# First up-projection slice of a SwiGLU kernel: from two hardware-queue loads to one load issued by GpSimd

## The chip, the cores and the metric

The kernel runs on one core of one Trainium2 chip. The metric is the device time of one execution in microseconds; of several executions the median is given. A profile is one execution taken by the hardware profiler. Its span runs from the first to the last instruction that the profile shows.

In the profile's lines, PE is TensorE (matmul), PEld its weight loads, DVE VectorE, ACT ScalarE, POOL GpSimd, SP SyncE. "SPq" and "ACTq" stand for an engine's issuing of transfers. `L195` is line 195 of the kernel before.

## The reference

```python
def reference(x, w_gate, w_up, w_down):
    g = _silu(x @ w_gate)
    u = x @ w_up
    return (g * u) @ w_down
```

x is 2048 x 640, w_gate and w_up are 640 x 1536, w_down is 1536 x 640, all bf16, and so is the output of 2048 x 640.

## The kernel before, in words

The 2048 rows are worked in four blocks of 512 (`NSB`, `S_BLK`). For a block, the gate and up projections come first, with the result transposed: the 1536 features lie on partitions in 12 tiles of 128 (`fc`), the 512 rows along the free dimension. One such tile is five matmuls for the gate (`pg`, over the five 128-row pieces `kd` of the inner dimension 640) and five for up (`pu`), both in `proj` (L195). `gate` then applies silu on ScalarE (L212) and multiplies on VectorE (L213) into `aT`. After 12 tiles the down projection runs from `aT` and `wd_sb` (L270 for the last 128 output columns, L299 for the first 512), and the results are stored. VectorE works out the last four rows of the output's inner products by itself (L148, `row_dots`) beside the other work.

The matmuls need x with its inner dimension on partitions (`xT`). Most of it comes through crossbar loads, transfers that transpose on their way (`turn_x`, L110, issued by SyncE, 512 rows at a time). The first 256 rows of block 0 (`PE_X` = 2 pieces of 128) come otherwise: they are loaded plainly into `x_sb` (L86), turned on TensorE with an identity matrix (L186), and copied to `xT` by ScalarE and VectorE (L191). The other 256 rows of block 0 come through the first crossbar load (L121 calls `turn_x(PE_X, SUB)`).

The weights come in slices of feature tiles, `W_CHUNKS` = (0, 2), (2, 4), (4, 8), (8, 12). The first slice of gate and up (256 columns, 320 KB each: 128 partitions x 5 pieces x 512 bytes) is split by `kd` at `K_CUT` = 2 between two queues, L115 to L120:

- gate, pieces 0 and 1 (128 KB): SyncE; pieces 2 to 4 (192 KB): ScalarE
- up, pieces 0 and 1 (128 KB): ScalarE; pieces 2 to 4 (192 KB): SyncE

After that SyncE issues, in this order: the first crossbar load, the remaining six weight slices (L83), w_down (L126), the crossbar load of block 1, and the transposed weights for VectorE's part. ScalarE goes on with its activation table and a first silu (L122).

`head` writes out the start of block 0. PE runs 18 small matmuls on ones (`warm`, L177), the ten transposes of x (L186), two more small matmuls, and then the gate matmuls of feature tiles 0 and 1 over the first 256 rows (L237, 14 of them: for pieces 0 and 1 in two halves of 128 rows, for pieces 2 to 4 over 256 rows). Then come the up matmuls of the same tiles and rows (L244, L245: ten, from `wu_sb`), and then, for each of the two tiles, the gate and up matmuls of the other 256 rows, which need the first crossbar load. From there on every tile is whole. `keep_order(engine)` ties each instruction of an engine to the one before it, in the order of the program; in `head` it is called for PE and ScalarE, at the end for VectorE and SyncE. GpSimd has only small memsets and the making of the identity (L71), at the very start.

`_trim` takes barriers out of the start and the end of the program and leaves the closing to SyncE.

Of the kernel before, what the change touches and what calls it, by code (L numbers as in the profile page):

```python
# [10 lines left out]
def _body(  # L11
# [8 lines left out]
    nc = tc.nc  # L20
# [12 lines left out]
    KD = D // P  # L33
# [10 lines left out]
    K_CUT = 2  # L44
    ROW_J = 0
    W_CHUNKS = [(0, 2), (2, 4), (4, 8), (8, 12)]
# [12 lines left out]
    wg_sb = consts.tile([P, KD, F], bf16)  # L59
    wu_sb = consts.tile([P, KD, F], bf16)  # L60
# [14 lines left out]
    wg_v = w_gate.rearrange("(kd p) f -> p kd f", p=P)  # L75
    wu_v = w_up.rearrange("(kd p) f -> p kd f", p=P)
    wd_v = w_down.rearrange("(kf p) d -> p kf d", p=P)

    def wslice(a, b):
        return slice(a * P, b * P)  # L80

    def load_w(eng, dst, src, a, b):
        eng.dma_start(out=dst[:, :, wslice(a, b)], in_=src[:, :, wslice(a, b)])  # L83
# [4 lines left out]
    def issue_order(a, b):  # L88
        tc.add_manual_dep(
            b,  # L90
            a.name,
            mybir.DependencyInfo(
                mybir.DependencyClass.NoSync, mybir.DependencyReason.DATA
            ),
            reason="issue_order",
        )

    def keep_order(engine):

        traced = [i for i in nc.cur_bb.bb.instructions if i.engine == engine]  # L100
        for a, b in zip(traced, traced[1:]):
            issue_order(a, b)
# [5 lines left out]
    def turn_x(c0, c1):  # L108
        s_sl = slice(c0 * P, c1 * P)
        nc.sync.dma_start_transpose(out=xT[:, :, s_sl], in_=xt_v[s_sl])  # L110
# [1 line left out]
    load_x(nc.sync, 0, 1)  # L112
    load_x(nc.scalar, 1, 2)
    f_sl = wslice(*W_CHUNKS[0])
    for dst, src, first, second in (  # L115
        (wg_sb, wg_v, nc.sync, nc.scalar),
        (wu_sb, wu_v, nc.scalar, nc.sync),
    ):
        for eng, k_sl in ((first, slice(0, K_CUT)), (second, slice(K_CUT, KD))):
            eng.dma_start(out=dst[:, k_sl, f_sl], in_=src[:, k_sl, f_sl])  # L120
    turn_x(PE_X, SUB)  # L121
    nc.scalar.activation(silu_first[:], ones[:, 0:1], ACT.Silu)  # L122
    for a, b in W_CHUNKS[1:]:
# [6 lines left out]
    def turn_w(dst, src):  # L130
# [7 lines left out]
        out=x_row[:],  # L138
        in_=x2[S - T : S, :].rearrange("t d -> (t d)").partition_broadcast(P),
# [35 lines left out]
    def warm(n):  # L175
        for _ in range(n):
            nc.tensor.matmul(  # L177
                pw[:, 0:P], lhsT=ones[:], rhs=ones[:], start=True, stop=True
            )

    def transpose_chunk(c, parts):
        c_sl = slice(c * P, (c + 1) * P)
        for copy, tag, k0, k1 in parts:
            pt = psum.tile([P, k1 - k0, P], bf16, tag=tag, name="pt")
            for kd in range(k0, k1):
                nc.tensor.transpose(  # L186
                    out=pt[:, kd - k0, :],
                    in_=x_sb[:, c, kd * P : (kd + 1) * P],
                    identity=ident[:],
                )  # L190
            copy(out=xT[:, k0:k1, c_sl], in_=pt[:])  # L191

    def proj(ps, w_sb, fc, sb, c0, c1):
        for kd in range(KD):
            nc.tensor.matmul(  # L195
                ps[:, c0:c1],
                lhsT=w_sb[:, kd, fc * P : (fc + 1) * P],
                rhs=xT[:, kd, sb * S_BLK + c0 : sb * S_BLK + c1],
                start=(kd == 0),
                stop=(kd == KD - 1),  # L200
            )

    def gu_tiles():
        pg = psum.tile([P, S_BLK], f32, tag="gu", name="pg", bufs=4)
        pu = psum.tile([P, S_BLK], f32, tag="gu", name="pu", bufs=4)
        return pg, pu

    def gate(pg, pu, sb, fc, n_s):

        s0 = sb * S_BLK  # L210
        sg = work.tile([P, S_BLK], f32, name="sg")
        nc.scalar.activation(sg[:, 0:n_s], pg[:, 0:n_s], ACT.Silu)  # L212
        nc.vector.tensor_tensor(  # L213
            out=aT[:, fc, s0 : s0 + n_s], in0=sg[:, 0:n_s], in1=pu[:, 0:n_s], op=ALU.mult
        )

    def head():

        dve, act = nc.vector.tensor_copy, nc.scalar.copy
        split = [(act, "po_a", 0, 2), (dve, "po_b", 2, KD)]
        late = PE_X * P
        (pg0, pu0), (pg1, pu1) = gu_tiles(), gu_tiles()
        warm(N_WARM)
        transpose_chunk(0, split)
        transpose_chunk(1, split)
        warm(N_GAP)  # L230
        early = [(kd, c * P, (c + 1) * P) for c in range(PE_X) for kd in range(K_CUT)]
        early += [(kd, 0, late) for kd in range(K_CUT, KD)]
        for kd, c0, c1 in early:
            for fc, pg in ((0, pg0), (1, pg1)):


                nc.tensor.matmul(  # L237
                    pg[:, c0:c1],
                    lhsT=wg_sb[:, kd, wslice(fc, fc + 1)],
                    rhs=xT[:, kd, c0:c1],  # L240
                    start=(kd == 0 and c0 == 0),
                    stop=(kd == KD - 1),
                )
        proj(pu0, wu_sb, 0, 0, 0, late)  # L244
        proj(pu1, wu_sb, 1, 0, 0, late)  # L245
        for fc, pg, pu in ((0, pg0, pu0), (1, pg1, pu1)):
            proj(pg, wg_sb, fc, 0, late, S_BLK)
            proj(pu, wu_sb, fc, 0, late, S_BLK)
            gate(pg, pu, 0, fc, S_BLK)
        keep_order(mybir.EngineType.PE)  # L250
        keep_order(mybir.EngineType.Activation)

    head()
    for sb in range(NSB):
        n_s = S_BLK if sb < NSB - 1 else S_BLK - T
# [26 lines left out]
        for q in range(P // Q):  # L282
            nc.scalar.dma_start(
                out=out2[
                    sb * S_BLK : sb * S_BLK + n_t, DA + q * Q : DA + (q + 1) * Q
                ].rearrange("(i r) c -> r i c", r=Q),
                in_=ot_q[q * Q : (q + 1) * Q, :].rearrange("r (i c) -> r i c", c=Q),
            )

        for j in range(SUB):  # L290
# [5 lines left out]
            for c0, c1, tag in cols:  # L296
# [10 lines left out]
                if c1 < D:  # L307
                    nc.scalar.copy(ot[:], po[:])  # L308
                    eng = nc.sync
                else:  # L310
                    nc.vector.tensor_copy(out=ot[:], in_=po[:])  # L311
                    eng = nc.scalar
# [81 lines left out]
def kernel(tc, *args):  # L394
    _body(tc, *args)
    tc.close()
    tc.compile()
    _trim(tc.nc)
# [30 lines left out]
```

## Time and profile before

| | us |
|---|---|
| median of 3 runs | 163.84 |
| lowest, highest | 163.25, 164.1 |
| span of the profiled execution | 162.2 |
| mean granted clock of TensorE in it, as recorded | 1.000 |

The span leaves out what lies around the program's instructions. So a step of the program is costed against the span, and what remains, 1.64 us between span and median, is carried over as it is.

The queues that the program uses, and the issuing of transfers at the start of SyncE (start, duration, what):

```profile
q1 hardware_dynamic: 33536, 14.72, 37.7%
q10 hardware_dynamic: 8896, 1.02, 4.1%
...
0.00 0.40 SPq L86 DMA_DIRECT2D x_sb<-in_x_dram  x1
0.46 0.42 SPq L120 DMA_DIRECT2D wg_sb<-in_w_gate_dram  x1
0.92 0.47 SPq L120 DMA_DIRECT2D wu_sb<-in_w_up_dram  x1
1.43 1.63 SPq L110 DMA_TRANSPOSE xT<-in_x_dram  x1
3.11 0.57 SPq L83 DMA_DIRECT2D wg_sb<-in_w_gate_dram  x1
```

q1 is SyncE's queue and q10 ScalarE's (packets, megabytes, share of the 16 DMA engines' time). An issue's duration is that of the issuing engine; the transfer lands later, and a separate view gives the time from issue to landing. No transfer goes through GpSimd.

### The profile page before, as it was taken

The page shows a single profiled execution, that of the slowest core. Times are in us where ns is not written, and L with a number is a line of the kernel's source. Part 1 is how long each engine was busy: PE and PEld are TensorE (multiplying, and loading weights), DVE is VectorE, ACT ScalarE, POOL GpSimd, SP SyncE. Part 2 cuts the span into 40 slices and gives each one's busy share as a digit, 9 for nine tenths or more (in the row PEclk, how much of TensorE's full clock was granted, in tenths as well). Part 3 has the DMA queues.
Part 4 walks back from the last instruction along what each step waited for, and adds up shares of the span by engine and source line. Part 5 has one row for each costly group of instructions (what it writes and reads, how often), then busy time and mean ns, then how long its engine had stood idle before and what let it go on. Part 6 is the DMA issues. An engine that isn't in the chain of part 4 may idle for free.

```text
span 162.2 us, 2118 instructions
## 1 busy us (share of the span) xinstructions
PE 159.8 (99%) x798; PEld 77.9 (48%) x798; DVE 110.9 (68%) x249; ACT 42.7 (26%) x74; POOL 0.6 (0%) x6
## 2 busy tenths in 40 slices
PE   9999999999999999999999999999999999999995
PEld 8854444444444444444444444444444444445454
DVE  2042233599469999979919999979964999993000
ACT  5132222112222222221222322221214222222121
POOL 1000000000000000000000000000000000000000
PEclk9999999999999999999999999999999999999999
DMA  7999999994179992003110000000320000000312
GB/s 208 258 339 348 362 218 249 219 234 94 34 185 178 224 195 61 4 0 34 65 65 0 0 4 2 0 0 2 63 69 32 0 0 0 0 0 4 50 39 73
DMA packets 42441, 15.86 MB, mean 98 GB/s; under 512 B 33216, under 2 KB 42304, under 8 KB 42432
## 3 DMA queue, kind: packets, MB, share of 16 engines
q1 hardware_dynamic: 33536, 14.72, 37.7%
q10 hardware_dynamic: 8896, 1.02, 4.1%
q8 instruction: 6, 0.10, 0.2%
q14 instruction: 3, 0.02, 0.1%
HBM read 6.88 MB, written 2.62 MB: 59 GB/s over the span
## 4 chain that ended last, share of the span: by engine, by line
PE 99%; DVE 0%; issue 0%
PE pu L195 32%; PE pg L195 31%; PE po_a L299 26%; PE po_t L270 6%; PE pw L177 1%; PE pg L237 1%; PE pt L186 1%; DVE ot_b L311 0%; DVE ones L106 0%
## 5 line engine op out<-in xcount | busy, mean ns | idle before, releaser
L195 PE MATMUL pu<-xT,wu_sb 128*128 128x512 bf16 (+2 forms) x250 | 59.8, 370 | 0.0
L195 PE MATMUL pg<-xT,wg_sb 128*128 128x512 bf16 (+2 forms) x240 | 58.5, 374 | 0.0
L213 DVE TENSOR_TENSOR aT<-sg,pu 128x512 bf16<-128x512 f32 (+1 forms) x48 | 32.8, 683 | 32.8 <-PE pu L195 28.1
L212 ACT ACTIVATE sg<-pg 128x512 f32<-128x512 f32 (+1 forms) x48 | 28.6, 596 | 71.2 <-PE pg L195 68.1
L299 PE MATMUL po_a<-wd_sb,aT 128*128 128x512 bf16 (+2 forms) x216 | 42.8, 358 | 0.0
L148 DVE SCALAR_TENSOR_TENSOR prod<-wgT,x_row 128x640 f32<-128x640 bf16 x48 | 39.4, 821 | 1.1
L148 DVE SCALAR_TENSOR_TENSOR prod<-wuT,x_row 128x640 f32<-128x640 bf16 x48 | 39.4, 822 | 1.0
L195 PEld LDWEIGHTS <-wu_sb 128*128 128x128 bf16 x250 | 24.4, 98 | 27.6 <-DMA wu_sb<-in_w_up_dram 0.3
L195 PEld LDWEIGHTS <-wg_sb 128*128 128x128 bf16 x240 | 23.5, 98 | 26.9
L299 PEld LDWEIGHTS <-aT 128*128 128x128 bf16 x216 | 20.7, 98 | 21.6
L308 ACT CAST ot<-po_a 128x512 bf16<-128x512 f32 (+1 forms) x17 | 9.5, 560 | 32.0 <-PE po_a L299 20.8
L270 PE MATMUL po_t<-aT,wd_sb 128*128 128x512 bf16 (+1 forms) x48 | 10.4, 366 | 0.0
L270 PEld LDWEIGHTS <-wd_sb 128*128 128x128 bf16 x48 | 4.7, 98 | 5.1
L311 DVE CAST ot_b<-po_a 128x128 bf16<-128x128 f32 x1 | 0.3, 291 | 9.9 <-PE po_a L299 9.9
L279 ACT CAST ot_t<-po_t 128x512 bf16<-128x512 f32 (+1 forms) x4 | 2.2, 558 | 11.6 <-PE po_t L270 11.6
L148 DVE DVE_READ_ACCUMULATOR prod<-wuT,x_row 128x1 f32 x48 | 3.9, 82 | 0.0
L148 DVE DVE_READ_ACCUMULATOR prod<-wgT,x_row 128x1 f32 x48 | 3.9, 82 | 0.0
L281 DVE STREAM_TRANSPOSE ot_q<-ot_t 128x512 bf16<-128x512 bf16 (+1 forms) x4 | 2.7, 678 | 1.7 <-ACT ot_t L279 1.7
L177 PE MATMUL pw<-ones 128*128 128x128 bf16 x20 | 2.5, 313 | 0.4 <-DVE ones L106 0.4
L191 DVE COPY xT<-pt 128x384 bf16<-128x384 bf16 x2 | 0.7, 358 | 2.9 <-PE pt L186 2.9
L237 PE MATMUL pg<-xT,wg_sb 128*128 128x128 bf16 (+1 forms) x14 | 2.3, 360 | 0.0
L177 PEld LDWEIGHTS <-ones 128*128 128x128 bf16 x20 | 2.1, 148 | 0.4 <-DVE ones L106 0.4
(15 smaller groups left out, 7.6 us busy)
## 6 DMA issues: line engine op xcount, KB each, us to landing
wd_sb<-in_w_down_dram SPq DMA_DIRECT2D x1, 1920.0 KB, 14.5
out_dram<-ot SPq DMA_DIRECT2D x15, 128.0 KB, 1.7
wg_sb<-in_w_gate_dram SPq DMA_DIRECT2D x2, 640.0 KB, 7.7
wu_sb<-in_w_up_dram SPq DMA_DIRECT2D x2, 640.0 KB, 8.7
x_row<-in_x_dram SPq DMA_DIRECT2D x1, 640.0 KB, 4.7
out_dram<-ot_q ACTq DMA_DIRECT2D x12, 32.0 KB, 1.9
wg_sb<-in_w_gate_dram SPq DMA_DIRECT2D x1, 320.0 KB, 4.9
wu_sb<-in_w_up_dram SPq DMA_DIRECT2D x1, 320.0 KB, 5.4
```

What stands on the lines that cost most here:

```text
L148: nc.vector.scalar_tensor_tensor(out=prod[:], in0=wT[:, fc, :], scalar=1.0, in1=x_row[:, t, :], op0=ALU.mult, op1=ALU.mult, accum_out=acc[ ...
L177: nc.tensor.matmul(pw[:, 0:P], lhsT=ones[:], rhs=ones[:], start=True, stop=True)
L186: nc.tensor.transpose(out=pt[:, kd - k0, :], in_=x_sb[:, c, kd * P : (kd + 1) * P], identity=ident[:],)
L195: nc.tensor.matmul(ps[:, c0:c1], lhsT=w_sb[:, kd, fc * P : (fc + 1) * P], rhs=xT[:, kd, sb * S_BLK + c0 : sb * S_BLK + c1], start=(kd == 0 ...
L212: nc.scalar.activation(sg[:, 0:n_s], pg[:, 0:n_s], ACT.Silu)
L213: nc.vector.tensor_tensor(out=aT[:, fc, s0 : s0 + n_s], in0=sg[:, 0:n_s], in1=pu[:, 0:n_s], op=ALU.mult)
L237: nc.tensor.matmul(pg[:, c0:c1], lhsT=wg_sb[:, kd, wslice(fc, fc + 1)], rhs=xT[:, kd, c0:c1], start=(kd == 0 and c0 == 0), stop=(kd == KD ...
L270: nc.tensor.matmul(po_t[:], lhsT=wd_sb[:, kf, DA:D], rhs=aT[:, kf, sb * S_BLK : sb * S_BLK + n_t], start=(kf == 0), stop=(kf == KF - 1),)
L279: nc.scalar.copy(ot_t[:], po_t[:])
L281: nc.vector.transpose(out=ot_q[:], in_=ot_t[:])
L299: nc.tensor.matmul(po[:], lhsT=aT[:, kf, s0 : s0 + P], rhs=wd_sb[:, kf, c0:c1], start=(kf == 0), stop=(kf == KF - 1),)
L308: nc.scalar.copy(ot[:], po[:])
```

## The change

The two loads of the first up slice, 128 KB from ScalarE and 192 KB from SyncE, go. One load of the whole slice, 320 KB, is issued by GpSimd, through `load_w`. The gate slice keeps its two loads on the same queues. On SyncE the crossbar load thereby directly follows the first part of the gate slice. In `head`, the order of GpSimd's instructions is now kept too, so that its load stands behind the making of the identity.

```diff
     load_x(nc.sync, 0, 1)
     load_x(nc.scalar, 1, 2)
     f_sl = wslice(*W_CHUNKS[0])
-    for dst, src, first, second in (
-        (wg_sb, wg_v, nc.sync, nc.scalar),
-        (wu_sb, wu_v, nc.scalar, nc.sync),
-    ):
-        for eng, k_sl in ((first, slice(0, K_CUT)), (second, slice(K_CUT, KD))):
-            eng.dma_start(out=dst[:, k_sl, f_sl], in_=src[:, k_sl, f_sl])
+    for eng, k_sl in ((nc.sync, slice(0, K_CUT)), (nc.scalar, slice(K_CUT, KD))):
+        eng.dma_start(out=wg_sb[:, k_sl, f_sl], in_=wg_v[:, k_sl, f_sl])
+    load_w(nc.gpsimd, wu_sb, wu_v, *W_CHUNKS[0])
     turn_x(PE_X, SUB)
     nc.scalar.activation(silu_first[:], ones[:, 0:1], ACT.Silu)
...
         keep_order(mybir.EngineType.PE)
         keep_order(mybir.EngineType.Activation)
+        keep_order(mybir.EngineType.Pool)
 
     head()
     for sb in range(NSB):
```

`load_w`, which the new line calls, is unchanged:

```python
    def load_w(eng, dst, src, a, b):
        eng.dma_start(out=dst[:, :, wslice(a, b)], in_=src[:, :, wslice(a, b)])
```

## The prediction

> **What bounds the kernel now.** I read the busy shares first, then the chain that ended last, then the chain of the first 7 us, and last the timeline and the transfers of that stretch. Busy time:
>
> ```profile
> span 162.2 us, 2118 instructions
> PE 159.8 (99%) x798; PEld 77.9 (48%) x798; DVE 110.9 (68%) x249; ACT 42.7 (26%) x74; POOL 0.6 (0%) x6
> PE 99%; DVE 0%; issue 0%
> ```
>
> TensorE is the bound from 0.40 us to the end, and the chain is PE for 99%. The change touches only loads of the first slices. So all that it can do is move the moment at which PE runs without waiting; what follows is a fixed train (five matmuls of 512 columns every 1.08 us). The chain of the first 7 us has no gap:
>
> ```profile
> 2.50 1.11 PE pt L186 x10
> 3.61 0.21 PE pw L177 x2
> 3.82 2.13 PE pg L237 x14
> 5.95 1.13 PE pu L195 x10
> ```
>
> The timeline gives the start of the same pieces (columns: start, duration, what, then idle time before it and what ended it):
>
> ```profile
> 3.61 2.34 PE L237 MATMUL pg<-xT,wg_sb 128*128 128x128 bf16 x14
> 5.80 1.01 PEld L195 LDWEIGHTS <-wu_sb 128*128 128x128 bf16 x10 [0.32 <-DMA wu_sb<-in_w_up_dram]
> 5.80 1.29 PE L195 MATMUL pu<-xT,wu_sb 128*128 128x256 bf16 x10
> 6.92 0.71 PE L195 MATMUL pg<-xT,wg_sb 128*128 128x256 bf16 x5
> ```
>
> PE's weight loader waited 0.32 us for the up slice, yet that is no 0.32 us to win. The last early gate matmul starts at 5.533, and its like are 0.213 apart, so the next could have started at 5.746 at the soonest. It started at 5.80: the real wait is 0.05 us. The clock explains the slow gate matmuls: a weight load takes 0.151 us up to 5.32 and 0.098 after 5.80 (the clock column shows full speed throughout and doesn't help). So the clock of this execution rose at about the moment at which the up slice arrived.
>
> What landed when (KB, microseconds from issue to landing; starts from the timeline):
>
> ```profile
> wg_sb<-in_w_gate_dram ACTq DMA_DIRECT2D x1, 192.0 KB, 3.6
> wu_sb<-in_w_up_dram SPq DMA_DIRECT2D x1, 192.0 KB, 4.7
> wu_sb<-in_w_up_dram ACTq DMA_DIRECT2D x1, 128.0 KB, 4.7
> xT<-in_x_dram SPq DMA_TRANSPOSE x1, 5.4
> ```
>
> Up: 0.92 + 4.7 = 5.62 and 1.04 + 4.7 = 5.74, needed at 5.746. Gate, second part: 0.57 + 3.6 = 4.17, needed by the ninth early matmul at 4.47. Crossbar load: 1.43 + 5.4 = 6.83, needed at 6.92. All three are just in time. The engines that carry them:
>
> ```profile
> 1.00:2.00 1.00, 1.00 (x13) 1.00 (x11) 0.00 (x0) 0.41 (x1) 0.00 (x0) 1.00 0.85 255
> 3.00:4.00 1.00, 1.00 (x12) 1.00 (x11) 0.71 (x2) 0.70 (x3) 0.00 (x0) 1.00 1.00 283
> 5.00:5.50 0.50, 0.50 (x4) 0.35 (x3) 0.00 (x0) 0.00 (x0) 0.00 (x0) 1.00 0.77 81
> ```
>
> The last two numbers are the share of the DMA engines and GB/s. They are full from 1 us on, but for a hole around 5.0 to 5.5. The packet records explain it: fifteen of the crossbar load's 256-byte packets, normally 18 ns, were held for 0.22 to 0.76 us and all let go at 5.33, when the one engine that was behind (its last up packet began at 5.12) had caught up.
>
> **The change part by part.** Two issues vanish: 0.47 us on SyncE (L120, at 0.92) and 0.51 on ScalarE (at 1.04). ScalarE's table load starts 0.5 earlier and its first copy (2.99) by up to 0.28, for which nobody waits: PE's own order, busy without a break, brings it to the first gate matmul only at 3.61. Worth 0. On SyncE the crossbar load starts at 0.92 instead of 1.43, and the six weight loads, w_down and everything behind move up by the same 0.51. These were in time already (the next gate slice: 3.11 + 4.9 = 8.01 against a use at 9.0; up: 3.73 + 5.4 = 9.13 against 10.0), so worth 0; should that cover be lost, the price is the lateness itself. GpSimd gains one load, kept behind the identity, which ends at 0.64 + 0.29 = 0.93. Nothing is queued behind it there. What hangs on it is PE: its order is written out, so while the ten up matmuls wait, everything waits, the late gate columns with them.
>
> So the sum is one term: when the up slice lands by the new way, against 5.74. The trace shows no load from GpSimd, hence bounds for each step:
>
> Writing its descriptors, 640 runs of 512 bytes. Low: SyncE's issue of the same shape (the next gate slice), 0.57 us. High: GpSimd's own pace, 0.293 us for 128 elements a partition (the identity's select), 2.3 ns each, for 640 reads and 640 writes in turn: 2.9. I take the two lists side by side, 640 x 2.3 ns = 1.5, since GpSimd's row is the nearest.
>
> Until the first packet: SyncE's first load was issued from 0.00 to 0.40 and its first packet ran at 1.0, so 0.6 after the issue. First up packet at 0.93 + 1.5 + 0.6 = 3.0 (2.1 to 4.4).
>
> Transfer, per engine: 40 up packets of 27 ns = 1.08. Behind its part of the gate slice SyncE's queue now has 80 crossbar packets of 18 ns, where it had 24 up packets. If the queues take turns, 40 of these run in between, 0.72, and the other half of the second gate part, 12 x 27 ns = 0.3: in all 2.1, to 5.15. Then the engine that is behind (0.45: the others ended at 4.65 to 4.70, it at 5.15) and the time from the last packet to landing (5.15 to 5.74, 0.6): **6.2**. With the early start more of the gate slice runs in between (2.65 instead of 2.1), and if no engine is behind that gives 2.1 + 2.65 + 0.6 = 5.35; with the late start the crossbar load is nearly done, and it is 4.4 + 1.2 + 0.45 + 0.6 = 6.7.
>
> The up matmuls then start at 6.2 + 0.06 = 6.26 instead of 5.80: **+0.46 us**; the ends are -0.05 (lands by 5.7) and +0.95. The second gate part may also be late by what the third queue takes, up to about 0.5 beyond 4.47, but this runs under the same wait (5.75 + 0.5 = 6.25) and isn't added. The crossbar load lands before 6.83 and is needed at 7.4: worth 0.
>
> The Trainium skill (DMA: Bandwidth & Descriptors, Anatomy of one DMA) gives a load from GpSimd about 2.0 us fixed plus its bytes at 436 GB/s; as an estimate, 0.93 + 2.0 + 0.75 = 3.7 for this one alone. By that the up slice would be in time and the sum would be -0.05 us; in the trace even a SyncE load of 160 KB to a nearly idle machine took 2.2, and the engines are full here, so I go by the rows.
>
> Span 162.2 + 0.46 = 162.7. The median of the runs, 163.84, lies 1.64 above the span, so **164.3 us**, +0.28%.
>
> **The rivals.**
>
> *Hidden anyway.* The software queue starts early, takes as many turns as the others, and the up slice lands by 5.75. For it: GpSimd is idle from 0.93, which is 4.8 us ahead of use. Against: the crossbar packets now compete with it. 163.8.
>
> *The software queue is late (the other side).* If descriptors cost both lists in turn at twice GpSimd's pace, 1280 x 4.6 ns = 5.9, and packets start only then, the slice lands at 0.93 + 5.9 + 0.6 + 1.08 + 0.6 = 9.1, +3.3 us. It is over the bound of 0.5% (0.82 us, about what a measurement of this kernel can tell from no change) from a landing at 6.6 on. A middle case, 7.4, gives +1.7: 165.5. For it: no row here shows GpSimd starting a transfer. Against: each of its rows is under 0.3 us.
>
> *The clock rises later.* It took PE 5.4 us of work to get it. A hole in PE's work ahead of that (the second gate part late, or an execution in which the clock would rise a little later) may delay it; if the whole count started again, 5.4 us at half speed would cost 2.7 us. Typical +1.5: 165.3. Against: in this execution it had all but risen by 5.75. The Trainium skill (TensorE: Matmul & The Clock Gate, What's actually happening) has a free-running window of 3.4 us that must be busy; by that a missed window costs 1.7 us, an estimate.
>
> *Both loads come earlier.* The hole in the transfers at 5.0 to 5.5 closes, up lands at 5.0 and the crossbar load at 6.0. Here it wins 0.05, as the gate matmuls end at 5.746. In an execution whose clock rises before 3.8, the gate matmuls would be over by about 4.9 (the second gate part lands at 4.17, six matmuls of 0.109 follow) and PE would win 5.80 - 5.0 = 0.8: 163.0. For it: runs from 163.25 to 164.1 differ by such an amount. Against: it needs a prompt software queue and an early clock in most runs.
>
> **How the numbers follow.** Forecast 0.50 (own range 163.8 to 164.9; 0.15 of it lies above 164.66); late queue 0.20; clock 0.10; hidden 0.10; both earlier 0.10, of which 0.08 by over 0.5%. Slower 0.15 + 0.20 + 0.10 = 0.45; faster 0.08; same 0.47. The range goes down to 163.2, into the last rival, and up to 166.0, into the two slow ones; about 0.05 is left out below and 0.1 above.
>
> **What would show it.** Right: the up matmuls' first weight load waits on the up slice until 6.0 to 6.7; SyncE's crossbar load is issued at 0.92 and lands ahead of 6.8; after the first up matmul the train runs unchanged. Wrong: no wait on the up slice (hidden), first packets of GpSimd's queue past 4.4 (late queue), weight loads of 0.151 us well past 5.8 (clock), a new wait in the early gate matmuls that lasts longer than the up slice, or a wait for the crossbar load at the late columns. A longer stretch after 9 us would refute the claim that only the head matters.

## The result and the profile after

The changed kernel took 172.59 us (median of four, 171.01 to 173.47) against 163.86 before (163.25 to 164.1): ratio 1.054, 95% interval 1.0501 to 1.058. The profiled execution's span grew from 162.2 to 169.7, by 7.5 us. I had forecast +0.46 and a range of 163.2 to 166.0. The profiled execution was the quickest of the four, whose spans on record are 169.7, 171.2, 171.4 and 172.2; what follows explains its 7.5 us, not the whole of the 8.7 between the medians.

From the page of the changed kernel: span, busy time, the software queue's line, and the shares of the chain that ended last.

```profile
span 169.7 us, 2106 instructions
PE 160.6 (95%) x786; PEld 78.5 (46%) x798; DVE 110.9 (65%) x249; ACT 42.9 (25%) x74; POOL 1.6 (1%) x7
q0 software_dynamic: 96, 0.33, 1.8%
PE 92%; DMA 6%; issue 1%; POOL 0%; DVE 0%; POOLq 0%
```

PE's busy time hardly moved; a DMA now holds 6% of the chain. The timeline says where (start, duration, what; in brackets the idle time before it and what ended it):

```profile
0.92 2.35 SPq L110 DMA_TRANSPOSE xT<-in_x_dram  x1
1.01 0.98 POOL L83 DMA_DIRECT2D wu_sb<-in_w_up_dram  x1
5.18 0.83 PE L234 MATMUL pg<-xT,wg_sb 128*128 128x256 bf16 x6 [0.24 <-DMA wg_sb<-in_w_gate_dram]
11.76 2.31 PE L192 MATMUL pu<-xT,wu_sb 128*128 128x256 bf16 x10 [5.75 <-DMA wu_sb<-in_w_up_dram]
13.87 1.27 PE L192 MATMUL pg<-xT,wg_sb 128*128 128x256 bf16 x5
```

The up matmuls start at 11.76 instead of 5.80. That is 5.96 us of the 7.5. Transfers of the first stage (KB, us from issue to landing):

```profile
wu_sb<-in_w_up_dram POOLq DMA_DIRECT2D x1, 320.0 KB, 10.7
wg_sb<-in_w_gate_dram ACTq DMA_DIRECT2D x1, 192.0 KB, 4.6
xT<-in_x_dram SPq DMA_TRANSPOSE x1, 11.1
```

The up slice lands at 1.01 + 10.7 = 11.7, and the crossbar load, issued half a microsecond earlier than before, lands at 0.92 + 11.1 = 12.0 instead of 6.83. Both are late, although GpSimd was done with its part at 1.99. By stretches (length, busy time of PE, PEld, DVE, ACT, POOL with counts; then the granted clock, the DMA engines' share, GB/s):

```profile
7.00:8.00 1.00, 0.00 (x0) 0.00 (x0) 0.00 (x0) 0.00 (x0) 0.00 (x0) 1.00 1.17 85
8.00:9.00 1.00, 0.00 (x0) 0.00 (x0) 0.00 (x0) 0.00 (x0) 0.00 (x0) 0.61 1.00 78
9.00:10.00 1.00, 0.00 (x0) 0.00 (x0) 0.00 (x0) 0.00 (x0) 0.00 (x0) 0.50 0.89 74
11.00:12.00 1.00, 0.24 (x2) 0.18 (x3) 0.00 (x0) 0.00 (x0) 0.00 (x0) 0.50 1.20 275
14.00:15.00 1.00, 1.00 (x7) 0.69 (x6) 0.00 (x0) 0.00 (x0) 0.00 (x0) 0.50 1.11 350
```

And one of the same stretches in the kernel before:

```profile
8.00:9.00 1.00, 1.00 (x12) 0.89 (x11) 0.69 (x1) 0.51 (x2) 0.00 (x0) 1.00 1.15 306
```

Two things are to be seen. The DMA engines count as 89 to 117% busy from 7 to 10 us, but move 74 to 85 GB/s, where the kernel before moved 291 to 348: packets are in flight and hardly move. And the clock of PE, which had nothing to do, falls to half at about 8.2 and stays there until 15.05. The up matmuls and what follows run from 11.76 to 15.05 at half speed, which loses (15.05 - 11.76) / 2 = 1.6 us. 5.96 + 1.6 is the 7.5 within 0.1.

The packet records of the trace show how they hang together. From 3.26 to 10.31 the crossbar load's 1280 packets of 256 bytes run; in the kernel before it took them from 4.10 to 6.29. In the middle, from 4.26 to 11.03, come the software queue's 80 packets. These are 4096 bytes long (eight runs of 512 packed together), while the hardware queues send each run of 512 by itself. Of the crossbar packets, 90 were held for over 0.1 us, up to 1.16; software packets took up to 1.88 us instead of 0.16. By 4.26, when the first software packet came, 408 of the crossbar packets were through.

### The profile page after: what moved, and what is told of

Read it like the earlier page. It is cut to its first block, busy times and chain, and to the rows that moved or that the text cites. A ratio compares the mean times of both kernels' runs of the same rounds, so it can differ in the third digit from the quotient of the medians.

```text
span 169.7 us, 2106 instructions
## 1 busy us (share of the span) xinstructions
PE 160.6 (95%) x786; PEld 78.5 (46%) x798; DVE 110.9 (65%) x249; ACT 42.9 (25%) x74; POOL 1.6 (1%) x7
## 4 chain that ended last, share of the span: by engine, by line
PE 92%; DMA 6%; issue 1%; POOL 0%; DVE 0%; POOLq 0%
PE pu L192 31%; PE pg L192 30%; PE po_a L297 25%; DMA wu_sb<-in_w_up_dram 6%; PE po_t L268 6%; DVE ot_b L309 0%; POOL ident masks.py:199 0%; POOL ident masks.py:197 0%; POOL const-float32-0.0 L411 0%; POOL const-uint8-127 L411 0%; POOLq L411 0%; POOL const-float32-1.0 L411 0%
## 5 line engine op out<-in xcount | busy, mean ns | idle before, releaser
L192 PE MATMUL pu<-xT,wu_sb 128*128 128x512 bf16 (+2 forms) x250 | 60.8, 376 | 5.7 <-DMA wu_sb<-in_w_up_dram 5.7
L192 PEld LDWEIGHTS <-wu_sb 128*128 128x128 bf16 x250 | 24.9, 100 | 33.8 <-DMA wu_sb<-in_w_up_dram 6.0
## 6 DMA issues: line engine op xcount, KB each, us to landing
wu_sb<-in_w_up_dram POOLq DMA_DIRECT2D x1, 320.0 KB, 10.7
```

The costliest lines, as they stand in the source:

```text
L192: nc.tensor.matmul(ps[:, c0:c1], lhsT=w_sb[:, kd, fc * P : (fc + 1) * P], rhs=xT[:, kd, sb * S_BLK + c0 : sb * S_BLK + c1], start=(kd == 0 ...
```

## The experiments

**Theory A**: a load by the software queue and a crossbar load in flight together hold each other up. **Theory B**: the software queue is slow by itself. **Theory C**: the crossbar load's earlier place is the cause, whatever carries the up slice. Three kernels part them, and a fourth measures the clock.

*The up slice on ScalarE's hardware queue, crossbar load at its new place.*

```diff
-    load_w(nc.gpsimd, wu_sb, wu_v, *W_CHUNKS[0])
+    load_w(nc.scalar, wu_sb, wu_v, *W_CHUNKS[0])
```

> The whole first up slice is one load on ScalarE's hardware queue; the crossbar load stands right behind SyncE's part of the gate slice as in the changed kernel; no transfer goes through GpSimd. Theory A (a software-queue load and a crossbar load in flight together hold each other up): the up slice lands by about 6 us, the wait on it stays under 0.6 us, span 162 to 163. Theory B (the software queue by itself is slow): the same, span 162 to 163. Theory C (the crossbar load's earlier place is the cause: it starves whatever carries the up slice): the up slice lands past 9 us, span 167 to 170.

Measured: 167.55 us against 163.30, ratio 1.019 (1.0121 to 1.026), span 166.5. Timeline, then transfers:

```profile
8.43 1.77 PE L192 MATMUL pu<-xT,wu_sb 128*128 128x256 bf16 x10 [2.52 <-DMA wu_sb<-in_w_up_dram]
```

```profile
wu_sb<-in_w_up_dram ACTq DMA_DIRECT2D x1, 320.0 KB, 7.4
xT<-in_x_dram SPq DMA_TRANSPOSE x1, 7.8
```

A and B both miss here: without any software queue, the up slice lands at 1.03 + 7.4 = 8.4 and PE waits 2.5 us. C is nearest, but misses too (a landing past 9 and a span from 167 were expected). So part of the loss comes with hardware queues alone, once the crossbar load runs beside the up slice instead of behind it: 4.3 of 7.5 us in the profiled executions, 1.9% of 5.4% by the ratios of the runs. Of the 4.3, 8.43 - 5.80 = 2.6 are the later start; the other 1.7 are the clock, which stood at half from 9.04 to 12.45. The four executions lie between 165.67 and 168.16, and the quickest has a mean clock of 1.00 on record where the others have 0.99. How much of the crossbar load's time here is plain sharing of the engines, the table below estimates.

*The crossbar load waits for the up slice (code shortened).*

```diff
-    turn_x(PE_X, SUB)
+    turn_load = turn_x(PE_X, SUB)
+    tc.add_manual_dep(turn_load, up_load.name, Sync)
```

> The changed kernel, but the first crossbar load, and with it all of SyncE's queue behind it, waits until GpSimd's up slice has landed. Theory A: with no crossbar load beside it the up slice lands at 4 to 6 us; PE then waits for the crossbar load instead (it needs about 3 to 5 us from its issue), span 165 to 168. Theory B: the up slice lands at 9 us or later just as in the changed kernel, the crossbar load after 12, span 173 or more. Theory C: as A.

Measured: 165.58 us once, span 164.2. Transfers, then the wait of PE:

```profile
wu_sb<-in_w_up_dram POOLq DMA_DIRECT2D x1, 320.0 KB, 4.1
xT<-in_x_dram SPq DMA_TRANSPOSE x1, 3.8
```

```profile
8.99 0.70 PE L202 MATMUL pg<-xT,wg_sb 128*128 128x256 bf16 x5 [2.30 <-DMA xT<-in_x_dram]
```

B falls. The software queue without the crossbar load beside it is prompt: first packet at 3.09, last at 4.6, landed at 1.01 + 4.1 = 5.1, which is 0.6 us earlier than the two hardware loads of the kernel before; the up matmuls start at 5.44. PE then waits 2.30 us for the crossbar load, which was issued only at 5.17. A and C have the landing right; the span lies under the 165 to 168 that both gave.

*The software queue carries the second up slice of the kernel before.*

```diff
-        load_w(nc.sync, wu_sb, wu_v, a, b)
+        load_w(nc.gpsimd if a == 2 else nc.sync, wu_sb, wu_v, a, b)
...
+        keep_order(mybir.EngineType.Pool)
```

> The kernel before, but its second up slice (feature tiles 2 and 3, the same 320 KB, needed at about 10 us) is loaded by GpSimd right behind the identity; the first up slice and the crossbar load are as before. Theory A: the crossbar load is held up though nothing that PE needs early comes by the software queue: it lands at 9 us or later instead of 6.83, PE waits for it at the late columns, span 165 to 171. Theory B: the crossbar load lands at 7 to 7.5; the second up slice lands at about 11.7 and PE waits for it by about 1 to 2 us, span 163 to 164.5. Theory C: no change, span 162 to 163.

Measured: 164.41 us once, span 163.1. The crossbar load landed at 1.42 + 6.3 = 7.7, the software load at 1.01 + 5.6 = 6.6. A's 9 us and B's 11.7 both miss; the span is nearest to B's, though B's reason is not. PE waited 1.45 us for the first up slice, which now shared the engines with the software queue. Here the software queue was in full flow (from 4.02) before the crossbar load's first packet (4.56), and was through at 5.9. By 5.5 us, 68 of the 80 software packets were through and only 115 of the 1280 crossbar packets, where in the changed kernel 408 crossbar packets ran ahead of the first software packet. So 71 software packets overlapped the crossbar load, and this did not set off the long hold-up: its packets took 2.6 us. That speaks against A as it was worded.

*The changed kernel with 70 small matmuls on ones between the gate and the up matmuls; their result isn't used.*

```diff
+    N_FILL = 70
...
+        pf = psum.tile([P, S_BLK], f32, tag="po_b", name="pf")
+        for _ in range(N_FILL):
+            nc.tensor.matmul(pf[:, 0:P], lhsT=ones[:], rhs=ones[:], start=True, stop=True)
         proj(pu0, wu_sb, 0, 0, 0, late)
```

> The changed kernel with 70 more small matmuls on ones between the early gate matmuls and the up matmuls, so that PE works on until about 10 us while it waits for the up slice (their result is not used). If the clock's fall during the wait costs what its half-speed stretch after 11.76 us suggests ((15.05 - 11.76) / 2 = 1.6 us), the up matmuls still start at about 11.7, each pair 0.109 us apart from the first on, and the span is 168.0 to 168.4 instead of 169.7. If the clock is of no account: 169.5 to 170.

Measured: 169.13 us once, span 167.8; the up matmuls start at 11.46 (0.3 earlier than in the changed kernel), and the ten take 1.26 us instead of 2.31 (1.29 in the kernel before):

```profile
11.46 1.26 PE L193 MATMUL pu<-xT,wu_sb 128*128 128x256 bf16 x10 [1.40 <-DMA wu_sb<-in_w_up_dram]
```

The gain of 1.9 us is the clock's 1.6 and the 0.3. The loss against the kernel before is now 5.6, and the late start alone is 11.46 - 5.80 = 5.66. The granted clock from 11 to 12 us is 1.00 here and 0.50 in the changed kernel. So the clock's share is shown; the span is 0.2 under the forecast, as the up slice came 0.3 earlier.

Theory A was then widened: any load in flight beside a crossbar load is held up and holds it up, the more so the longer its packets (P). The next kernels test the length, with hardware queues only, and the time of overlap.

*640 KB beside the crossbar load of the kernel before, in runs of 512 bytes, and in runs of 5120 bytes.* In the first, ScalarE issues the second gate and up slices right behind its part of the first up slice, in the second the load of the last rows; SyncE issues these no more.

```diff
     turn_x(PE_X, SUB)
+    load_w(nc.scalar, wg_sb, wg_v, 2, 4)
+    load_w(nc.scalar, wu_sb, wu_v, 2, 4)
...
-    for a, b in W_CHUNKS[1:]:
+    for a, b in W_CHUNKS[2:]:
```

> The kernel before (all on hardware queues, order of the first slices unchanged), but ScalarE issues the second gate and up slices (640 KB in runs of 512 bytes) right behind its part of the first up slice, so that they are in flight beside the crossbar load. Theory P (a transfer beside the crossbar load holds it up by its packets' length): crossbar load lands at 8 to 9.5 us instead of 6.83, packets beside it are short. Theory S (only the software queue does it): lands at 6.8 to 7.6, the plain sharing of the engines.

```diff
     turn_x(PE_X, SUB)
+    nc.scalar.dma_start(
+        out=x_row[:],
+        in_=x2[S - T : S, :].rearrange("t d -> (t d)").partition_broadcast(P),
+    )
...
-    nc.sync.dma_start(
-        out=x_row[:],
-        in_=x2[S - T : S, :].rearrange("t d -> (t d)").partition_broadcast(P),
-    )
```

> The kernel before, but ScalarE issues the load of the last rows, 640 KB in long runs of 5120 bytes, at the same place (right behind its part of the first up slice) instead of SyncE later; as many bytes beside the crossbar load as in the run with 512-byte runs. Theory P: the crossbar load lands later than in that run by 1 us or more (10 us or later). Theory S: the same as in that run, within 0.5 us.

Measured: 167.95 us and 173.08 us, once each. The crossbar load, first with runs of 512, then of 5120 bytes beside it:

```profile
xT<-in_x_dram SPq DMA_TRANSPOSE x1, 8.3
```

```profile
xT<-in_x_dram SPq DMA_TRANSPOSE x1, 13.2
```

It lands at 1.42 + 8.3 = 9.7 with the short packets and at 1.43 + 13.2 = 14.6 with the long ones, and at 6.83 without either. Equal bytes, the same queue, no software: S, that only the software queue does it, falls, and the order is P's, though the first landing lies 0.2 past its range. Each is a single run, and the two loads differ in one more thing: the one of long runs reads the same 5120 bytes for every partition. A load of distinct long runs was not tried. (In the first of the two, ScalarE's longer issuing also delayed its copies, and PE waited 1.40 us for these; that is in its time, not in the landing.)

*The software load in two halves of 128 columns.*

```diff
-    load_w(nc.gpsimd, wu_sb, wu_v, *W_CHUNKS[0])
+    load_w(nc.gpsimd, wu_sb, wu_v, 0, 1)
+    load_w(nc.gpsimd, wu_sb, wu_v, 1, 2)
```

> The changed kernel, with the software load cut into one of 128 columns for each feature tile (runs of 256 bytes instead of 512, the same bytes). If a software packet is eight runs, packets are 2048 bytes, and by theory P the up slice lands earlier than in the changed kernel, at 8 to 10 us; if a packet is filled up to 4096 bytes, the up slice lands at 11 to 12 us again, the first half at 7 to 9.

Measured: 168.06 us once, span 166.8. Packets were filled up to 4096 bytes (two of those and one of 2048 for each engine and load), yet the up matmuls started at 8.87, not past 11. So P's forecast for filled packets missed: the length of the packets alone doesn't set the price. Why two halves with nearly the same packets start the up matmuls 2.9 us earlier stays open.

*The crossbar load waits for less: SyncE's part of the gate slice, ScalarE's piece of x, SyncE's piece of x.* The edit is that of the second experiment with another load in the place of `up_load`. All three were compared with the kernel before.

> The changed kernel, but SyncE's crossbar load waits until SyncE's own part of the gate slice has landed (about 3.3 us), so that its first packets come at about 4.6, when the software queue's packets have just run out (4.5 in the run in which the crossbar load waited for the up slice). Theory A, now widened (any load in flight beside a crossbar load is held up, and holds it up; the software queue's 4096-byte packets more than 512-byte ones): up lands at 5.1 to 5.8, crossbar load at 7 to 7.6, PE waits for it under 1 us, span 162 to 163.2. Rival (what costs is that the software queue shares the engines with the second gate part, not the overlap with the crossbar load): up lands past 8, span over 166.

Measured: 164.07 against 163.43, ratio 1.0031 (1.0015 to 1.0047). The up slice landed at 1.02 + 4.3 = 5.3, the crossbar load at 3.75 + 3.6 = 7.4, and PE waited 0.74 us for the latter, all as A gave it. The rival falls: the software queue still shares the engines with the second gate part here.

> The changed kernel, but SyncE's crossbar load waits until ScalarE's piece of x has landed (about 2.75 us) instead of being issued at 0.92: its first packets then come at about 4.1, while the software queue still has a quarter of its packets (it runs from 3.0 to 4.75 with nothing beside it). Theory A: a short overlap costs little: up lands at 5.3 to 6, the crossbar load at 6.5 to 7.2, time within 0.4% of the kernel before either way, 162.9 to 164.1. If even a short overlap sets off the long hold-up: up past 7, time over 165.5.

Measured: 163.65 against 163.37, ratio 1.0008 (0.9988 to 1.0029).

> As the run that waits for ScalarE's piece of x, but waiting for SyncE's own piece (about 2.35 us): first crossbar packets at about 3.7, in the middle of the software queue's. Theory A: a longer overlap, up lands at 6 to 8, time 164 to 167, between the run above and the changed kernel. Without a link between overlap and time: as the run above.

Measured: 163.63 against 163.37, ratio 1.0008 (0.9983 to 1.0033). The timeline and transfers of the middle one (waiting for ScalarE's piece of x):

```profile
2.95 1.96 SPq L110 DMA_TRANSPOSE xT<-in_x_dram  x1
5.55 1.26 PE L200 MATMUL pu<-xT,wu_sb 128*128 128x256 bf16 x10 [0.27 <-DMA wu_sb<-in_w_up_dram]
6.88 0.70 PE L200 MATMUL pg<-xT,wg_sb 128*128 128x256 bf16 x5
```

```profile
wu_sb<-in_w_up_dram POOLq DMA_DIRECT2D x1, 320.0 KB, 4.5
xT<-in_x_dram SPq DMA_TRANSPOSE x1, 3.9
```

Issuing the crossbar load 2 us later than in the changed kernel takes away all of the loss; the two loads landed at 1.02 + 4.5 = 5.5 and 2.95 + 3.9 = 6.9, as A gave it. The last of the three missed its forecast of 164 to 167: issued at 2.68, its first crossbar packet still ran only at 4.37, when 54 of the 80 software packets were through (63 in the middle run, at 4.35), so it doesn't test a longer overlap. None of the three beats the kernel before.

*The reverse order: GpSimd's load waits for the crossbar load (code shortened).*

```diff
+    turn_load = turn_x(PE_X, SUB)
     up_load = load_w(nc.gpsimd, wu_sb, wu_v, *W_CHUNKS[0])
+    tc.add_manual_dep(up_load, turn_load.name, Sync)
```

> The changed kernel with the order turned round: the crossbar load is issued at 0.92 as in the changed kernel, and GpSimd's up load waits until it has landed. Beside the crossbar load then run only the second gate part and, behind it on the same queue, SyncE's next slices. Theory A: the crossbar load, at its early place, isn't slow by itself: it lands at 5.0 to 6.5 us instead of 12.0; up lands 4 to 7 us later (it meets plain loads only), span 165 to 169, less than the changed kernel's 169.7 although the two now run one after the other. Rival (the early place itself makes the crossbar load slow): it lands past 8, span over 172.

Measured: 172.66 us once, span 171.4. Timeline and transfers:

```profile
5.50 0.98 POOL L83 DMA_DIRECT2D wu_sb<-in_w_up_dram  x1 [4.56 <-DMA xT<-in_x_dram]
```

```profile
wu_sb<-in_w_up_dram POOLq DMA_DIRECT2D x1, 320.0 KB, 8.1
xT<-in_x_dram SPq DMA_TRANSPOSE x1, 4.3
```

The crossbar load at its early place is quick by itself: landed at 0.91 + 4.3 = 5.2, its packets through in 1.6 us (3.11 to 4.72). So C in its plain form falls too: it takes the pair. The span missed (165 to 169 expected): the software load, written by 6.48, sent its first packet only at 10.1, with SyncE's weight slices filling the engines meanwhile, and landed at 13.6. The two loads one after the other in this order cost more than both at once.

Put together from the packet records, the crossbar load's time from its first to its last packet. "Own" is an estimate: what all packets that touch this stretch would take one engine if none were held (a sixteenth of their sum, at 18 ns for 256 bytes, 27 for 512, 84 for 2048, 159 for 4096, 196 for 5120).

```
kernel                          in flight beside it                        us          own
reverse order                   512-byte packets, at its start             1.6         1.8
waits for the up slice          512-byte packets, at its end               1.9         1.6
waits for gate / x pieces       0 to 26 of 4096 bytes, at its start        1.8 to 2.0  1.5 to 1.7
before                          512-byte packets, at its start             2.2         2.1
second up slice by GpSimd       71 of 4096 bytes, flowing before it began  2.6         2.4
up slice on ScalarE             512 bytes, throughout                      3.6         2.6
second slices on ScalarE        512 bytes, throughout                      3.9         3.0
software load in two halves     4096 and 2048, from 0.6 us after its start 4.5         2.4
changed kernel                  4096 bytes, from 1.0 us after its start    7.0         2.6
changed, with fill matmuls      4096 bytes, from 0.2 us after its start    7.3         2.8
last rows on ScalarE            5120 bytes, from 0.3 us after its start    10.0        3.7
```

Beside 512-byte packets the crossbar load takes 1 us more than the packets' own time, so most of its 3.6 and 3.9 us is plain sharing. In the changed kernel it takes 4.4 us more, beside the last rows 6.3. But long packets are not enough by themselves. In the four kernels in which they began after the crossbar load's first packet, it took 2.0 to 6.3 us more than its own time; in the three in which they began before it (the second up slice by GpSimd, and the waits for the two pieces of x), 0.1 to 0.4. So what came first made the difference in these runs; why it does is not shown.

The records also show how the crossbar load moves. In the changed kernel its 90 held packets let go in 19 groups, those of a group within 0.04 us, and from 5.55 to 8.97 us one group follows the next after 0.19 to 0.27. The commonest length of a software packet there is 0.19 us. With the fill matmuls and with the last rows on ScalarE most steps are 0.19 to 0.25 us too. So the crossbar load goes forward in steps of about one long packet. The records don't name the engines, so which engine a step waited for is not shown.

## Why the prediction was wrong

*What bounds the kernel* was right: from the up matmuls on, the train runs at the same pace, and the whole loss sits before 15.05 us. That there was at most 0.05 us to win on the wait holds for that one execution alone: where the early gate matmuls took 1.90 and 1.63 us instead of 2.34, the up matmuls began at 5.44 and 5.40 (crossbar load waiting for the up slice, and for the gate piece). The packets held until 5.33 were nineteen, not fifteen.

*Things put at 0.* ScalarE's earlier issues brought nothing, as said. SyncE's did not come for nothing: the crossbar load's move to 0.92, which put it under way before the up slice, was worth 0 in the sum, and holding it back to 2.95 took the whole loss away. The crossbar load "lands before 6.83 and is needed at 7.4: worth 0" was wrong: it landed at 12.0. It cost little by itself only because the up slice was as late.

*Writing the descriptors*, 1.5 us (0.57 to 2.9): 0.98 measured. *First packet* at 3.0 (2.1 to 4.4): 4.26 in the changed kernel, 3.35 in the fill run, whose transfers are the same, and 3.09 with no crossbar load in flight. Only the size was off here, and the range held it.

*Transfer, per engine* is the step that failed: "If the queues take turns, 40 of these run in between, 0.72". I added up packet times as if an engine that serves one queue were free for the next a packet later, 2.1 us in all. (The 40 up packets of 27 ns were 5 of 4096 bytes on each engine, 0.8 to 1.0 us unheld instead of 1.08; that term was not what failed.) Measured: the crossbar packets took 7.0 us and the software packets 6.8, for about 2.4 us of packet time on each engine (80 x 18 ns and 5 x 0.16 to 0.19 us); the slice landed at 11.7 instead of 6.2. The runs show in its place that the two loads hold each other up across the engines when the software packets come in behind the crossbar load's first, and that it then goes on in steps of about one long packet: keeping them apart by making the crossbar load wait takes the loss away, and without the up slice beside it the crossbar load at its early place takes 1.6 us. I had the row of the packets that let go together at 5.33, and charged it once, as an engine that is behind (0.45), instead of for every turn. That the price grows with the packets' length rests on two single runs, 3.9 us beside 512-byte packets and 10.0 beside 5120, and on the changed kernel's 7.0 between them; the two halves (4.5) and the second up slice by GpSimd (2.6) don't fit a rule of length alone.

*The rivals.* "The software queue is late" had the side right but not the mechanism: writing descriptors was quicker than I had it, and the queue without the crossbar load beside it is prompt. "The clock rises later" had its size right, 1.5 typical against 1.6 shown, but not its way: the clock had risen in time, at 4.8, and fell during the wait. That the two sizes are alike is chance. I named no rival in which the two loads held each other up, the one place where the change put something new beside something else.

*Page against row.* The Trainium skill (DMA: Bandwidth & Descriptors, Anatomy of one DMA) gave 3.7 us for the landing of this load alone, an estimate; the run that came nearest to alone landed at 5.1. The Trainium skill (DMA: Bandwidth & Descriptors, Queues, rings and completion order) says that each DMA engine goes round its queues by packets; the 4096-byte packets beside the 256-byte ones are in the trace, and no run here shows the order of turns on one engine.

What stays open: why the overlap in the run with the second up slice (software packets in flow before the crossbar load began) cost so little, while the same packets coming in behind its first cost so much; why two halves did better; what delays a software load's first packet when the engines are full (1.1 us from descriptors written with the gate slice beside it, 2.3 in the changed kernel, 1.4 with the fill matmuls, 3.6 in the reverse order); and which engine a held crossbar packet waited for.

## What to carry to other kernels

In this kernel a crossbar load was not one more transfer that takes its share: a load beside it was held up with it, on the software queue and on a hardware queue, and longest where long packets came in behind its first one. So ask of any load that moves what will now run beside a crossbar load, and whether the two can be kept apart by a place in a queue or by a wait; the wait has a price too, as the reverse order shows (span 171.4). A load through GpSimd landed 4.1 us after its issue with neither a crossbar load nor a backlog of weights beside it, against 4.7 for the two hardware loads that it replaced; behind such a backlog it took 8.1.

## What the runs showed of the hardware that I had not expected

The software queue packs 512-byte runs into packets of 4096 bytes; the hardware queues send them one by one. GpSimd writes the 640 runs in 0.98 us. PE's clock fell to half after about 2.2 us without work (6.0 to 8.2), and in the clock records of the changed kernel it stood at full speed for 3.41 us, then at half for 6.83 (10.24 in the run with long packets on ScalarE), all multiples of 3.41. So a wait can cost more than its length, 1.6 us more here, and whether it does isn't told by its length alone: with the up slice on ScalarE the clock fell at 9.04, after a wait of 2.5 us that had ended at 8.43, and in the run in which the crossbar load waited for the up slice a wait of 2.30 us left it at full speed. The 3.41 us agree with the free-running 3.4 us window of the Trainium skill (TensorE: Matmul & The Clock Gate, What's actually happening). The Trainium skill has the clock fall there after at least one idle window; here 2.2 us without work were enough.
